# Loading q of the last three batches as zero-padded token rows and transposing it by DMA from SBUF

## The chip, the cores and the metric

The kernel runs on one core of one Trainium2 chip. The metric is the device time of one execution in microseconds (us). Times are medians of several runs; the profile is of one further execution, taken by the hardware profiler.

## What is computed

Eight batches of eight heads, 576 tokens, head size 64: attention in which a token sees itself and the 63 tokens before it. The result, 4608 tokens by 512 columns, goes through two matrix products with a function between them.

```python
scores = scale * np.matmul(q, k.transpose(0, 1, 3, 2))
mask = (rel >= 0) & (rel < window)          # window = 64
attn = softmax of np.where(mask, scores, -1e9)
x = np.matmul(attn, v)                      # rearranged to (4608, 512)
h = x @ w_in                                # 512 -> 2048
g = h - np.tanh(h)
out = g @ w_out                             # 2048 -> 512
```

## The kernel before

**Tiling.** A pair g is two heads of one batch (g = 4b + pair, pairs 0 to 31). A batch is cut into nine windows of 64 tokens; a window of queries meets 128 keys. The dense part works on nine chunks of 512 tokens. A batch has 576 tokens, so chunk c needs parts of batches c-1 and c. All of PSUM is one tile of eight banks: 0 to 2 hold the dense products, 3 the transposes, 4 the scores, 5 to 7 the products with v (for batch 0, banks 0, 1 and 7 serve otherwise too).

**The order is written out.** `PLAN` is a list of some 1300 words; each calls one function of the table `STEPS`, and what it issues goes into the queue of its engine in that order. An engine takes its instructions strictly in the order of the list, and waits at the first whose data or buffer isn't ready. Words that matter here (the last letter of some is the engine: v VectorE, a ScalarE, p GpSimd):

- `H.c.m` four products of 512 columns into one bank (L487), `A.c.m` tanh (L495, ScalarE), `G.c.m` the subtraction (L501, VectorE), which frees the bank. In chunk 0 `H.0.m` uses bank m mod 3, in chunk 1 (m+1) mod 3, later m mod 2.
- `W.c.s.p` four products with w_out (L526); 128 tokens s take four of them. `O.c.s` copies the result out of PSUM (L88 or L90) and stores it by a DMA from the SP queue (L542). The last 128 tokens are done in two halves of the columns (L519, L537).
- `Rp.g.n.4` three score products of 128 columns for three windows into bank 4 (L300), `Rx.g.n.4` exp of them (L305, ScalarE), `M.g` masking (L393, VectorE), `PP.g` the products with v for two pairs (L418), `DR` and `DN` their normalization (L426, L435, L438).
- Batches 0 to 2 bring k to the layout that `Rp` needs by PE: a load, a cast (`ck`), six transposes (`Fp`, L261), a copy out of PSUM (`Fc`). For q the same: `cq`, `Ep.g.3`, and two copies `Ea`, `Eb` (64 partitions each, L88 or L90), since q lies in a buffer padded with zeros so that one product serves both heads. Transposes and their copies share bank 3.
- Batches 3 to 7 load k as token rows, `lr.b.i.h` (L176): block i of 128 tokens (the fifth has 64), four heads h; `tk.b.i` (L181) then transposes the block by DMA from SBUF, issued by SP.
- q of batches 3 to 7 is loaded by one DMA per batch, `LQ.b` (L114). Batches 3, 4 and 5 go through PE (`cq`, `Ep`, `Ea`, `Eb`). Batches 6 and 7 go, per pair, through `cz.g` (two copies on GpSimd into a zeroed tile, L128), `bo.g` (a DMA to a DRAM buffer, L133) and `td.g` (a DMA transpose from DRAM, L138).
- `LV.b.i` loads v (L160), `Z.b` copies it across partitions (L166, L167). `Y.b` transposes the attention's result into the dense part's input by two DMAs (L472); for batches 0 to 2 PE does it (`Xp`, `Xc`).
- `wi` and `wo` load the weights (L189, L197); `U` is a product on zeros, `N` puts the mask into bank 6 (L245).

**Queues.** GpSimd issues all loads with a cast; SP issues the outputs, the DMA transposes and the bounce. The transposed q has two buffers (pairs g mod 2).

Of the kernel before, what the change touches and what calls it, by code (L numbers as in the profile page):

```python
# [15 lines left out]
def kernel(  # L16
# [69 lines left out]
    def move(eng, o, i):  # L86
        if eng is nc.scalar:
            nc.scalar.activation(o, i, ACT.Copy)  # L88
# [35 lines left out]
    def cast_q(g):  # L124

        i = stage.pop((g, "q")).rearrange("p h (e d) -> p h e d", d=D)
        for h in range(2):
            nc.gpsimd.tensor_copy(qz[g % 2][:, h, :, 64 * h:64 * h + 64], i[:, h])  # L128

    def bounce(g):  # L130

        t = dram.tile([2, S, 128], BF16, tag="q", name="qd")
        nc.sync.dma_start(out=t.rearrange("h (p e) c -> p h (e c)", e=E),  # L133
                          in_=qz[g % 2].rearrange("p h e c -> p h (e c)"))
        rows[g, "qd"] = t

    def tr_dma(g):
        nc.sync.dma_start(out=qT[g % NR].rearrange("c h s -> c (h s)"),  # L138
                          in_=rows.pop((g, "qd")).rearrange("h s c -> (h s) c"), transpose=True)
# [414 lines left out]
    def subtract(c, m, s=None):  # L554
# [18 lines left out]
        P=pv, D=norm, PP=pv_pairs, DR=recip_pairs, DN=norm_pairs, Xp=x_tr, Xc=x_put, Y=x_dma,  # L573
        H=first_layer, A=tanh, G=subtract, W=yp_mm, O=y_out)

    def play(script):
# [16 lines left out]
        H.0.6 Rp.4.1.4 G.0.4 A.0.6 Fc.6.3.a G.0.6 wo.2 wo.3 H.0.8 cq.6.v lq.9.p H.0.7 lk.9.p cq.7.v H.0.9 A.0.8  # L593
        G.0.8 A.0.7 lv.1.3.0 G.0.7 Ep.7.3 A.0.9 G.0.9 H.0.11 Eb.7.3.a Rx.4.1.4 A.0.11 za.1.0.v lv.1.2.0 Ea.7.3.v
        lv.1.2.1 H.0.10 H.0.12 lv.1.3.1 Rp.7.2.4 G.0.11 lr.3.3.0 A.0.10 lk.10.p G.0.10 Ep.6.3 A.0.12 Eb.6.3.a
        lq.11.p Ea.6.3.a G.0.12 H.0.14 A.0.14 H.0.13 LV.2.1 Rx.7.2.4 M.4 H.0.15 lk.11.p Rp.6.0.4 M.5 Rx.6.0.4
        PP.4 G.0.14 A.0.15 lq.10.p zb.1.3.p cq.8.v LQ.3 DR.4 G.0.15 Rp.7.0.4 LV.2.0 Rx.7.0.4 W.0.0.0 Rp.6.2.4
        A.0.13 DN.4.0 W.0.0.1 ck.8.v Ep.8.3 Rx.6.2.4 Rp.6.1.4 Rx.6.1.4 LV.2.3 Ea.8.3.v Eb.8.3.v G.0.13 W.0.1.0
        M.6 W.0.0.2 Rp.7.1.4 W.0.1.1 DN.4.1 Fp.8.3 W.0.1.2 W.0.0.3 LV.2.2 Rx.7.1.4 lr.3.3.1 cq.9.v Fc.8.3.a
        Rp.8.2.4 Rx.8.2.4 O.0.0.v Ep.9.3 Ea.9.3.a Eb.9.3.a W.0.1.3 W.0.2.0 O.0.1.a ck.9.v Fp.9.3 M.7 Rp.8.0.4  # L600
        W.0.2.1 Rx.8.0.4 W.0.3.0 DN.4.2 lr.3.2.1 Fc.9.3.a zb.1.2.v Xp.1.0.0.3 za.1.2.v lr.3.4.1 Xc.1.0.0.3.a
        Rp.9.2.4 za.1.3.v ck.10.v PP.6 lr.3.1.0 DR.6 Xp.1.0.1.3 DN.6.1 lr.3.4.0 tk.3.3 LV.2.4 DN.6.2 lr.3.1.1
# [103 lines left out]
```

## Time and profile before

| | us |
|---|---|
| median of 3 runs (315.44 to 316.02) | 315.92 |
| profiled execution, its own time | 314.95 |
| span of its trace | 313.3 |
| PE busy | 302.4 (97%) |
| VectorE busy | 187.8 (60%) |
| ScalarE busy | 171.2 (55%) |
| GpSimd busy | 108.6 (35%) |
| granted TensorE clock | 0.998 |

Busy times are unions of an engine's instructions within the span; the time outside the span (some 1.7 us) belongs to the start and the end of the execution. Matmuls are pipelined: four products of 512 columns are shown as 1.03 us when they stand alone, but follow each other every 0.86 us.

### The profile page before, as it was taken

To read this page: it belongs to the slowest core of one execution; us is meant where nothing else is said; L and a number is where in the kernel's file an instruction comes from. 1 tells how busy PE (TensorE), PEld (TensorE's weight loads), DVE (VectorE), ACT (ScalarE), POOL (GpSimd) and SP (SyncE) were. 2 spreads that over 40 slices of the span, in tenths; PEclk is the share of its full clock that TensorE was granted. 3 is DMA by queue.
4 is the path that set the end of the run, shared out by engine and by line. 5 is a ranking of instruction groups with operands and counts; after the bars stand their busy time and mean duration, and the time that the engine had idled before them with its cause. 6 is when DMAs were issued, how large, how long until landed. Compare 5 with 4: busy or idle time off the path is not lost.

```text
span 313.3 us, 6081 instructions
## 1 busy us (share of the span) xinstructions
PE 302.4 (97%) x2385; PEld 165.0 (53%) x2413; DVE 187.8 (60%) x327; ACT 171.2 (55%) x320; POOL 108.6 (35%) x160
## 2 busy tenths in 40 slices
PE   6988999999999999999999999999999999999995
PEld 2564565656655555555555455555554444444444
DVE  3685988699758785667556555873774534343300
ACT  3576875489866767657454536445333533433311
POOL 8990666686739442293441640000000000000000
PEclk9999999999999999999999999999999999999999
DMA  9999999999999999997999999481005110010111
GB/s 158 149 181 203 170 208 137 192 138 141 142 116 151 143 156 159 127 132 170 175 183 165 181 193 175 113 180 36 35 36 116 59 37 33 33 37 33 67 69 67
DMA packets 113133, 39.11 MB, mean 125 GB/s; under 512 B 96336, under 2 KB 107600, under 8 KB 113104
## 3 DMA queue, kind: packets, MB, share of 16 engines
q0 software_dynamic: 72064, 18.06, 67.1%
q1 hardware_dynamic: 41040, 20.65, 30.5%
q8 instruction: 19, 0.31, 0.4%
q14 instruction: 10, 0.08, 0.1%
HBM read 36.70 MB, written 11.80 MB: 155 GB/s over the span
## 4 chain that ended last, share of the span: by engine, by line
PE 87%; DMA 5%; POOL 5%; issue 1%; ACT 0%; POOLq 0%; ACTq 0%
PE ps L487 39%; PE ps L526 37%; PE ps L300 4%; PE ps L418 3%; DMA xT<-xs 3%; DMA wi<-in_moe_w_in_dram 3%; PE ps L261 2%; POOL kall L108 1%; POOL vw L160 1%; POOL qall L108 1%; PE ps L519 1%; PE ps L453 1%; POOL vw L147 0%; POOL seen L241 0%; ACT ysb L88 0%
## 5 line engine op out<-in xcount | busy, mean ns | idle before, releaser
L501 DVE TENSOR_TENSOR gT<-ps,th 128x512 bf16<-128x512 f32 x144 | 97.3, 687 | 81.9 <-ACT th L495 81.2
L487 PE MATMUL ps<-xT,wi 128*128 128x512 bf16 x576 | 141.7, 379 | 1.1 <-DMA wi<-in_moe_w_in_dram 0.7
L526 PE MATMUL ps<-w_out_sb,gT 128*128 128x512 bf16 x532 | 131.8, 379 | 1.4
L495 ACT ACTIVATE th<-ps 128x512 f32<-128x512 f32 x144 | 84.6, 597 | 77.8 <-PE ps L487 75.6
L487 PEld LDWEIGHTS <-wi 128*128 128x128 bf16 x576 | 62.0, 113 | 50.4 <-DMA wi<-in_moe_w_in_dram 0.9
L526 PEld LDWEIGHTS <-gT 128*128 128x128 bf16 x560 | 53.0, 98 | 56.9
L305 ACT ACTIVATE pt<-ps 128x384 bf16<-128x384 f32 (+2 forms) x92 | 45.8, 504 | 20.3 <-PE ps L300 19.0
L176 POOL DMA_DIRECT2D kall<-in_k_dram x50 | 37.2, 758 | 28.2 <-DMA kw<-kall 19.9
L160 POOL DMA_DIRECT2D vw<-in_v_dram x35 | 31.1, 894 | 10.8 <-PE ps L418 8.6
L88 ACT ACTIVATE ysb<-ps 128x512 f32<-128x512 f32 (+1 forms) x23 | 13.3, 579 | 28.4 <-PE ps L526 25.9
L393 DVE TENSOR_TENSOR pt<-pt,ps 128x1152 bf16<-128x1152 bf16 x28 | 20.6, 745 | 2.7 <-ACT pt L305 2.7
L300 PEld LDWEIGHTS <-kw 128*128 128x128 bf16 x180 | 14.4, 98 | 11.7 <-issue 0.3
L88 ACT ACTIVATE qt<-ps 64x576 bf16<-64x576 bf16 x30 | 19.3, 642 | 1.3 <-PE ps L300 0.3
L300 PE MATMUL ps<-qt,kw 128*128 128x128 bf16 x180 | 19.0, 219 | 0.0
L128 POOL COPY qz<-qall 96x384 bf16<-96x384 bf16 x16 | 7.6, 528 | 24.9 <-DMA qd<-qz 11.6
L438 DVE TENSOR_TENSOR xs<-ps,rcp 128x384 bf16<-128x384 f32 x28 | 14.9, 548 | 0.1
L225 PE MATMUL ps<-warm 128*128 128x512 bf16 x26 | 9.3, 496 | 2.2 <-DVE warm L206 2.1
L90 DVE COPY ysb<-ps 128x512 f32<-128x512 f32 x14 | 9.6, 685 | 3.1 <-PE ps L526 3.1
L418 PEld LDWEIGHTS <-pt 128*64 128x64 bf16 x504 | 9.2, 112 | 3.0 <-issue 1.3
L418 PE MATMUL ps<-vw,pt 128*64 128x65 bf16 x504 | 10.7, 197 | 0.0
L261 PE MATMUL ps<-ident,qb 96*128 96x96 bf16 x132 | 9.3, 206 | 1.0 <-DVE qb L90 1.0
L261 PEld LDWEIGHTS <-qb 96*128 96x128 bf16 x132 | 7.5, 97 | 4.5 <-DVE qb L90 1.9
(69 smaller groups left out, 165.4 us busy)
## 6 DMA issues: line engine op xcount, KB each, us to landing
out_dram<-ysb SPq DMA_DIRECT2D x35, 256.0 KB, 2.2
vw<-in_v_dram POOLq DMA_DIRECT2D x28, 128.0 KB, 5.3
qall<-in_q_dram POOLq DMA_DIRECT2D x5, 576.0 KB, 8.7
kall<-in_k_dram POOLq DMA_DIRECT2D x40, 64.0 KB, 4.8
qd<-qz SPq DMA_DIRECT2D x8, 288.0 KB, 3.3
w_out_sb<-in_moe_w_out_dram POOLq DMA_DIRECT2D x4, 512.0 KB, 8.4
kall<-in_k_dram POOLq DMA_DIRECT2D x11, 144.0 KB, 4.7
qall<-in_q_dram POOLq DMA_DIRECT2D x11, 144.0 KB, 4.6
```

The costliest lines, as they stand in the source:

```text
L88: nc.scalar.activation(o, i, ACT.Copy)
L160: nc.gpsimd.dma_start(out=w[:, 2 * i + 1, :, 0:D] if i < NF else w[64:128, 2 * i, :, 0:D], in_=v[b, :, 128 * i:128 * i + n].rearrange("h p ...
L176: nc.gpsimd.dma_start(out=token_rows(b)[0:c, i, :, h, :], in_=k[b, NP * h:NP * h + NP, 128 * i:128 * i + c].rearrange("r p d -> p r d"))
L261: nc.tensor.transpose(tp[:, e, :], src[:, e, :], ident[:P, :P])
L300: nc.tensor.matmul(sp[:, i], kt[:, 64 * j:64 * j + 128], qT[g % NR][:, :, 64 * j:64 * j + 64], start=first, stop=first or i == n - 1)
L305: nc.scalar.activation(PT[g % NPT][:, js[0]:js[0] + len(js), :].rearrange("p i (h t) -> p i h t", h=2), sp, ACT.Exp, scale=scale)
L393: nc.vector.tensor_tensor(p, p, mask.unsqueeze(1).to_broadcast([128, 2 * NJ, 64]), ALU.mult)
L418: nc.tensor.matmul(ps[r, bank, 65 * i:65 * i + 65], PT[(g + r2) % NPT][:, j, r], vw[b % 2][:, j, p0 + r2 + NP * h, :], start=True, stop=True)
L487: nc.tensor.matmul(hp, w_in_tile(ki, m), chunk_tile(c)[:, n.start // 64:n.stop // 64, ki % 2, 64 * (ki // 2):64 * (ki // 2) + 64], start=( ...
L495: nc.scalar.activation(th[:, n], hp, ACT.Tanh)
L501: nc.vector.tensor_tensor(gT[c][:, m, columns(s)], hp, th, ALU.subtract)
L526: nc.tensor.matmul(yp, gT[c][:, m, s * 128:(s + 1) * 128], w_out_sb[:, m, :], start=n == 1 and i == 0, stop=n == 4 and i == 3)
```

## The change

1. q of batches 5, 6 and 7 takes one path. `Lq.b.half.i` (30 DMAs by GpSimd) loads a block of 128 tokens, four heads, into every second half of zeroed rows; `tq.b.two.i` (30 DMA transposes by SP) turns a block of two pairs into the padded layout. `LQ.5` to `LQ.7`, `cq`, `Ep`, `Ea`, `Eb` of pairs 20 to 23, and `cz`, `bo`, `td` of pairs 24 to 31 go, with the DRAM buffer.
2. The transposed q has four buffers, one for each pair of a batch, in one tile; the rows of q have one buffer. Two more memsets (`mq.2`, `mq.3`).
3. The zeroing `z` is in five words, one for each block of rows: 128x1024 bf16 each in place of two of 96x1536.
4. P.2 writes banks 0 and 1; its normalization is in three instructions (`DS.2`, `DH.2.0`, `DH.2.1`) in place of two.
5. The last 128 tokens are cut into 128 and 384 columns, the 384 last, in place of two halves of 256.
6. The list is as it was up to `D.2`, and in a new order from there. One of the nine `U` words is dropped, and the engine of some copies and casts is another.

```diff
-    qT = [const.tile([128, 2, S], BF16, name=f"qt{i}") for i in range(NR)]
+    q_two = const.tile([128, NP, 2, S], BF16, name="qt0")
+    qT = [q_two[:, i] for i in range(NP)]
+    q_rows = const.tile([128, NF + 1, NP, 2, 128], BF16, name="qr0")
-    qz = [const.tile([P, 2, E, 128], BF16, name=f"qz{i}") for i in range(2)]
...
+    def load_q_rows(b, half, i):
+        c = min(128, S - 128 * i)
+        nc.gpsimd.dma_start(out=q_rows[0:c, i, :, half, 64 * half:64 * half + 64],
+                            in_=q[b, NP * half:NP * half + NP, 128 * i:128 * i + c].rearrange("r p d -> p r d"))
+    def tr_q(b, two, i):
+        c = min(128, S - 128 * i)
+        nc.sync.dma_start(out=q_two[:, 2 * two:2 * two + 2, :, 128 * i:128 * i + c].rearrange("p r h c -> p (r h) c"),
+                          in_=q_rows[0:c, i, 2 * two:2 * two + 2].rearrange("p r h d -> p (r h d)"), transpose=True)
...
     def more_zeros(i):
-        nc.vector.memset(qz[i], 0.0)
+        nc.vector.memset(q_rows[:, i], 0.0)
...
     def pv_banks(g):
-        return ps[:, 4:8:3, :] if g < NP and g % 2 and not BY_HEAD else ps[:, 5:7, :]
+        return ps[:, 0:2, :] if g == 2 else ps[:, 5:7, :]
...
+    def norm_sums(g):
+        ov = pv_banks(g)[:, :, 0:5 * (D + 1)].rearrange("p n (i c) -> p n i c", c=D + 1)
+        last[g] = sm_pool.tile([128, 2, 5, 1], F32, tag="rc", name="rc")
+        nc.vector.reciprocal(last[g], ov[:, :, :, D:D + 1])
+    def norm_half(g, n):
+        b, pr = divmod(g, NP)
+        k = 5 - n
+        ov = pv_banks(g)[:, n, 0:k * (D + 1)].rearrange("p (i c) -> p i c", c=D + 1)
+        nc.vector.tensor_tensor(xs[b % 2][:, 5 * n:5 * n + k, pr, :], ov[:, :, 0:D],
+                                last[g][:, n, 0:k].to_broadcast([128, k, D]), ALU.mult)
...
+    def last_columns(half):
+        n = 3 * d_model // 4
+        return slice(0, n) if half else slice(n, d_model)
```

The stretches of the list that the prediction speaks of, before and after. First, where the dense part begins:

```diff
-        Rx.5.0.4 lv.1.0.1 lv.1.0.0 Xp.0.0.0.3 Rp.5.1.4 D.2 Xc.0.0.0.3.a U.1.2 Xp.0.1.0.3 Xp.0.1.1.2 Rx.5.1.4
-        Xc.0.1.1.2.v U.1 mq.0 Rp.5.2.4 Xc.0.1.0.3.a H.0.1 A.0.1 H.0.0 ck.7.v Rx.5.2.4 G.0.1 H.0.2 wo.0 za.1.1.p
-        lq.8.p A.0.0 G.0.0 A.0.2 Ep.4.3 H.0.4 Eb.4.3.a wo.1 Ea.4.3.a A.0.4 ck.6.v G.0.2 H.0.3 Fp.7.3 Rp.4.2.4
-        lk.8.p H.0.5 A.0.3 N Fc.7.3.v zb.1.0.p Rx.4.2.4 G.0.3 Fp.6.3 A.0.5 zb.1.1.p Rp.4.0.4 Rx.4.0.4 G.0.5
+        Rx.5.0.4 lv.1.0.1 lv.1.0.0 Xp.0.0.0.3 Rp.5.1.4 DS.2 DH.2.0 DH.2.1 Xc.0.0.0.3.a U.1.2 Xp.0.1.0.3
+        Xp.0.1.1.2 Rx.5.1.4 Xc.0.1.1.2.v U.1 mq.0 lq.8.p N mq.3 Rp.5.2.4 mq.2 Xc.0.1.0.3.a lk.8.p Ep.4.3 ck.7.v
+        Rx.5.2.4 Ea.4.3.a ck.6.v H.0.1 A.0.1 Eb.4.3.a H.0.0 A.0.0 G.0.0 H.0.2 z.4 A.0.2 Rp.4.2.4 z.2 Rx.4.2.4
+        Rp.4.0.4 G.0.1 za.1.1.p Rx.4.0.4 wo.1 H.0.3 Fp.7.3 H.0.4 wo.0 G.0.2 cq.7.v A.0.3 Rp.4.1.4 wo.2 Rx.4.1.4
+        Fc.7.3.v Fp.6.3 A.0.4 H.0.5 G.0.3 A.0.5 lq.9.p G.0.4 H.0.6 zb.1.1.p Fc.6.3.v G.0.5 H.0.7 Ep.7.3 A.0.6
+        G.0.6 A.0.7 Ea.7.3.a wo.3 Eb.7.3.a H.0.8 lv.1.3.0 A.0.8 H.0.9 zb.1.0.p A.0.9 lk.9.p cq.6.v Rp.7.2.4
+        lv.1.3.1 G.0.7 G.0.8 Ep.6.3 G.0.9 H.0.10 Ea.6.3.a Rx.7.2.4 lv.1.2.0 M.5 A.0.10 G.0.10 cq.8.a Eb.6.3.v
+        lv.1.2.1 H.0.11 H.0.12 A.0.11 G.0.11 H.0.13 Ep.8.3 lk.11.p A.0.12 Eb.8.3.a LV.2.1 Rp.6.0.4 za.1.0.v
+        G.0.12 M.4 H.0.14 H.0.15 A.0.14 G.0.14 PP.4 Rx.6.0.4 ck.8.a W.0.0.0 Ea.8.3.v Rp.7.0.4 W.0.0.1 DR.4
```

Second, the first transposes of batches 5 and 6 (only the words of the SP and GpSimd queues and a few of PE are kept):

```
SP:     O.2.0 tq.5.0.1 tq.5.0.4 tk.5.1 tq.5.0.3 tk.5.4 tq.5.0.0 tk.5.0 tq.5.0.2 tk.6.2 tq.5.1.4 O.2.1 tq.5.1.3
        tq.5.1.1 tq.5.1.2 tq.5.1.0 Y.4 O.2.2 tq.6.0.1 tk.6.4 O.2.3 tq.6.0.2 tq.6.1.2 tk.6.1 O.3.0 tq.6.0.3
        tk.6.0 tq.6.1.0 tq.6.0.0 tq.6.1.3 O.3.1 tq.6.1.1 tq.6.1.4 tq.6.0.4 tk.6.3 Y.5 O.3.2
GpSimd: lr.7.1.1 LV.5.2 LV.5.4 lr.6.0.0 lr.6.0.1 Lq.6.0.0 LV.5.0 LV.5.3 Lq.6.0.1 Lq.6.0.2 LV.6.3 lr.6.1.0
        lr.6.4.1 Lq.6.1.1 Lq.6.1.2 lr.7.4.0 lr.6.3.1 lr.6.1.1 Lq.6.1.3 Lq.6.0.3
```

Third, the end:

```diff
-        W.8.0.2 G.8.15 W.8.1.2 W.8.0.3 W.8.1.3 O.8.0.a W.8.2.0 W.8.2.1 W.8.2.2 W.8.2.3 W.8.3.2 O.8.1.a W.8.3.3
-        O.8.2.a W.8.3.0 W.8.3.1 O.9.0.a O.8.3.a"""
+        G.8.15 W.8.0.0 W.8.0.1 W.8.0.2 W.8.0.3 W.8.1.1 W.8.1.2 O.8.0.a W.8.1.3 O.8.1.a W.8.2.0 W.8.2.1 W.8.2.2
+        W.8.2.3 O.8.2.v W.8.3.0 W.8.3.1 W.8.3.2 O.8.3.a W.8.3.3 O.9.0.a"""
```

More of the change, by code (lines that the diff above doesn't have):

```diff
@@ L109, in load, with load_q @@
         stage[g, n] = t
-    def load_all(b, n):
-        t = rows_all[n][b % 2][0:P]
-        nc.gpsimd.dma_start(out=t, in_=(q if n == "q" else k)[b].rearrange("h (p e) d -> p h (e d)", e=E))
+    def load_q(b):
+        t = rows_all["q"][b % 2][0:P]
+        nc.gpsimd.dma_start(out=t, in_=q[b].rearrange("h (p e) d -> p h (e d)", e=E))
         for pr in range(NP):
-            stage[b * NP + pr, n] = t[:, pr::NP]
+            stage[b * NP + pr, "q"] = t[:, pr::NP]
     def cast(g, n, eng=nc.gpsimd):
@@ L122, in cast @@
         rows[g, n] = t
[L124 to L139, printed above, removed]
+    def load_q_rows(b, half, i):
[6 more added lines that the diff above has]
+                          in_=q_rows[0:c, i, 2 * two:2 * two + 2].rearrange("p r h d -> p (r h d)"), transpose=True)
     def load_v_tail(b, eng=nc.gpsimd):
@@ L271, in put @@
             r = slice(64 * h, 64 * h + 64)
-            move(eng, qT[g % NR].rearrange("c h (p e) -> c h p e", e=E)[r, h], t[r])
+            move(eng, qT[g % NP].rearrange("c h (p e) -> c h p e", e=E)[r, h], t[r])
     def group(g, grp, bank):
@@ L299, in scores @@
         for i, j in enumerate(js):
-            nc.tensor.matmul(sp[:, i], kt[:, 64 * j:64 * j + 128], qT[g % NR][:, :, 64 * j:64 * j + 64],
+            nc.tensor.matmul(sp[:, i], kt[:, 64 * j:64 * j + 128], qT[g % NP][:, :, 64 * j:64 * j + 64],
                              start=first, stop=first or i == n - 1)
@@ L447, in norm @@
         nc.vector.tensor_tensor(xo[:, :, :, pr, :], ov[:, :, :, 0:D], rc.to_broadcast([128, 2, 5, D]), ALU.mult)
+    last = {}
+    def norm_sums(g):
[8 more added lines that the diff above has]
+                                last[g][:, n, 0:k].to_broadcast([128, k, D]), ALU.mult)
     def x_tr(b, half, part, bank):
@@ L514, in yp_mm @@
             half = part // 2
-            d = slice(half * (d_model // 2), (half + 1) * (d_model // 2))
+            d = last_columns(half)
             n = turn(c, s, half)
@@ L532, in y_out @@
             c, s = NC - 1, 3
-            d = slice(half * (d_model // 2), (half + 1) * (d_model // 2))
+            d = last_columns(half)
             ysb = sm_pool.tile([128, d_model], F32, tag="ysb", name="ysb")
@@ L558 @@
         i=make_ident, u=make_warm, mv=pads_v, mt=pads_k, mq=pads_q, mk=pads_kw, U=warm_up, h=make_hide, n=make_mask, N=put_mask,
-        z=lambda: [more_zeros(i) for i in range(2)],
+        z=more_zeros,
         lk=lambda g, e: load(g, "k", e), lq=lambda g, e: load(g, "q", e),
-        LK=lambda b: load_all(b, "k"), LQ=lambda b: load_all(b, "q"),
+        LQ=load_q, Lq=load_q_rows,
         lt=load_v_tail, lv=load_v, LV=load_rows,
@@ L593 @@
[L593 to L602, printed above, removed]
@@ new lines @@
+        Xc.1.0.0.3.a za.1.2.v W.0.2.2 PP.6 Xp.1.0.1.3 DR.6 DN.6.0 lr.3.3.0 lr.3.2.1 DN.6.2 ck.10.v ck.11.a
+        Rx.9.2.4 Xc.1.0.1.3.a W.0.3.0 W.0.3.1 lr.3.4.0 Xp.1.1.0.3 Xc.1.1.0.3.a z.1 W.0.2.3 cq.10.a DN.6.1
+        Xp.1.1.1.3 Rp.8.0.4 W.0.3.2 Rx.8.0.4 Rp.9.1.4 Xc.1.1.1.3.v Rx.9.1.4 tk.3.2 Ep.10.3 LV.2.4 H.1.0 A.1.0
+        Ea.10.3.v O.0.2.v G.1.0 W.0.3.3 Eb.10.3.a lr.3.1.0 H.1.1 Fp.10.3 Rp.8.1.4 cq.11.a lr.3.1.1 A.1.1 O.0.3.v
+        Rx.8.1.4 Fc.10.3.a Z.2 H.1.2 H.1.3 A.1.2 A.1.3 G.1.1 G.1.2 lr.3.0.1 Fp.11.3 Rp.9.0.4 H.1.4 G.1.3
@@ new lines @@
+        Rx.9.0.4 M.8 A.1.4 M.9 Fc.11.3.a lr.3.0.0 Rp.10.2.4 Rx.10.2.4 tk.3.3 tk.3.1 G.1.4 z.3 lr.3.4.1 H.1.5
+        H.1.6 Rp.10.0.4 Ep.11.3 A.1.5 lr.5.2.1 LV.3.2 A.1.6 Eb.11.3.a G.1.5 H.1.7 Ea.11.3.a H.1.8 cq.14.v G.1.6
+        Rx.10.0.4 A.1.7 LV.3.4 LV.3.1 lr.4.3.0 cq.13.v Rp.10.1.4 PP.8 A.1.8 G.1.7 cq.12.a Rx.10.1.4 LQ.4 H.1.9
+        Ep.12.3 Rp.11.1.4 A.1.9 LV.3.0 lr.4.3.1 G.1.8 DR.8 Rx.11.1.4 Ea.12.3.a DN.8.2 LV.3.3 H.1.10 G.1.9
+        Eb.12.3.a tk.3.4 H.1.11 DN.8.0 A.1.10 lr.4.0.1 Rp.11.0.4 H.1.12 A.1.11 Ep.13.3 lr.4.2.0 cq.15.v
@@ new lines @@
+        Rx.17.2.4 Rp.16.2.4 Ea.19.3.a O.1.3.a M.17 Z.4 Rx.16.2.4 H.2.14 lr.5.0.0 A.2.13 lr.5.1.1 Rp.16.1.4
+        W.2.0.0 lr.7.2.1 A.2.14 Rx.16.1.4 G.2.13 W.2.0.1 Eb.19.3.v G.2.14 tk.5.3 Rp.18.1.4 H.2.15 A.2.15
+        Lq.5.1.4 W.2.0.2 G.2.15 lr.6.2.0 Rx.18.1.4 H.3.0 H.3.1 lr.5.0.1 A.3.0 Rp.18.0.4 G.3.0 W.2.0.3 H.3.2
+        A.3.1 Rx.18.0.4 Rp.19.1.4 M.16 Lq.5.0.3 G.3.1 O.2.0.a lr.5.4.1 H.3.3 A.3.2 PP.16 lr.6.4.0 Rx.19.1.4
+        Rp.18.2.4 Lq.5.0.0 A.3.3 tq.5.0.1 G.3.2 DR.16 H.3.4 G.3.3 A.3.4 W.2.1.0 Lq.5.1.2 Rx.18.2.4 M.18 tq.5.0.4
@@ new lines @@
+        tq.6.0.4 DR.22 A.4.11 DN.22.2 DN.22.0 Lq.7.1.1 G.4.10 H.4.12 G.4.11 W.3.2.3 DN.22.1 Rp.25.0.3 tk.6.3
+        H.4.13 Rx.25.0.3 A.4.13 A.4.12 Y.5 O.3.2.v Lq.7.1.4 LV.6.1 W.3.3.0 Rp.24.1.3 Lq.7.0.3 Lq.7.0.1 G.4.12
+        W.3.3.1 W.3.3.2 Rx.25.1.4 Rp.24.0.4 G.4.13 Rx.24.0.4 H.4.15 H.4.14 A.4.15 A.4.14 Rp.26.2.4 W.3.3.3
+        LV.6.0 G.4.15 Rx.24.1.3 lr.7.0.1 Rx.26.2.4 H.5.1 G.4.14 O.3.3.a Rp.25.2.3 LV.7.0 Rx.25.2.3 lr.7.1.0
+        Rp.24.2.4 Lq.7.1.3 Rx.24.2.4 W.4.0.0 M.24 H.5.0 A.5.0 W.4.0.1 W.4.0.2 LV.6.2 Lq.7.0.4 G.5.0 W.4.0.3
@@ new lines @@
+        G.5.8 M.27 tk.7.4 H.5.10 LV.7.3 tq.7.0.4 PP.26 tq.7.0.2 G.5.11 A.5.10 G.5.10 O.4.2.a tq.7.1.3 H.5.13
+        A.5.13 DR.26 DN.26.1 H.5.12 W.4.3.0 W.4.3.1 DN.26.2 W.4.3.2 DN.26.0 LV.7.2 A.5.12 LV.7.1 G.5.12 LV.7.4
+        Y.6 H.5.14 W.4.3.3 G.5.13 Rp.29.2.3 O.4.3.a H.5.15 Z.7 Rp.29.1.4 A.5.14 Rx.29.1.4 G.5.14 W.5.0.0
+        Rx.29.2.3 W.5.0.1 tq.7.1.1 Rp.29.0.3 A.5.15 H.6.0 G.5.15 H.6.1 Rx.29.0.3 A.6.0 Rp.28.0.4 A.6.1 W.5.0.2
+        Rp.28.1.3 G.6.0 G.6.1 H.6.2 Rx.28.0.4 H.6.3 M.29 Rx.28.1.3 Rp.28.2.4 tq.7.1.0 A.6.2 W.5.0.3 G.6.2
```

132 lines of the change are left out of this document (57 added, 75 removed).

## The prediction, on record before the result

> **What bounds the kernel.** I read the page first: busy times, slices, the chain that ended last.
>
> ```profile
> PE 302.4 (97%) x2385; PEld 165.0 (53%) x2413; DVE 187.8 (60%) x327; ACT 171.2 (55%) x320; POOL 108.6 (35%) x160
> ...
> PE   6988999999999999999999999999999999999995
> ...
> ACT  3576875489866767657454536445333533433311
> ...
> PEclk9999999999999999999999999999999999999999
> ...
> PE 87%; DMA 5%; POOL 5%; issue 1%; ACT 0%; POOLq 0%; ACTq 0%
> ```
>
> PE is busy in every slice after the third, at full clock, and holds 87% of the chain. A busy matmul can hide waits, so I also added up PE's work along the list: four 512-column products 0.865 us (rows of L487 and L526 that follow each other), three score products 0.17, a pair of pairs in L418 0.90, six transposes 0.26. From 26.0 us, when the dense part begins, this gives 309.7 for the last matmul; the trace has 309.8. So PE has under 1 us of waits after 26 us: anything that adds a wait there is paid in full. The timeline shows where it begins and its largest later wait:
>
> ```profile
> 26.00 2.78 PE L487 MATMUL ps<-xT,wi 128*128 128x512 bf16 x12 [0.72 <-DMA wi<-in_moe_w_in_dram]
> 27.09 0.60 ACT L495 ACTIVATE th<-ps 128x512 f32<-128x512 f32 x1 [1.83 <-PE ps L487]
> ...
> 29.44 1.30 ACT L88 ACTIVATE qt<-ps 64x576 bf16<-64x576 bf16 x2
> ```
>
> ```profile
> 110.80 0.42 PE L261 MATMUL ps<-ident,qb 96*128 96x96 bf16 x6
> ...
> 118.13 1.92 PE L487 MATMUL ps<-xT,wi 128*128 128x512 bf16 x8 [0.27 <-DMA xT<-xs]
> ```
>
> The first line is the wait for w_in; the last is H.3 waiting for Y.3, whose DMA was issued at 109.42 and landed 8.7 us later.
>
> **The change, part by part.**
>
> *PE work.* Four Ep words go: six transposes begin at 110.80 and the next product at 111.06, so 4 x 0.26 = 1.04. One U of 512 columns goes: 0.22. Ep.4 (0.26) and N (0.13, 32.17 to 32.30) move ahead of H.0.1, into the wait that ends at 26.00. Sum: -1.65 us. The casts, copies and bounces that go were beside PE's work, and cost nothing.
>
> *Y.3.* DN.14, which it needs, comes 1.3 us earlier in PE's positions, and H.3 0.6 earlier; GpSimd stands still before it (lr.7.2.1 waits for tk.5.2), so fewer loads are in flight. The wait of 0.27 and the restart of a drained pipe (four products 1.03 instead of 0.86) go: -0.44.
>
> *The first chunk, 26 to 45 us.* New waits. H.0.1, H.0.0, H.0.2 end at 28.59, Rp.4.2 at 28.76. The next word on PE, Rp.4.0, writes the same bank 4 with nothing between (before, three words lay between). It waits for Rx.4.2 on ScalarE, which stands behind A.0.1, Eb.4, A.0.0 and A.0.2: 27.09 + 0.60 + 0.65 + 0.60 + 0.60 + 0.49 = 30.03. Wait: 1.3. Then Rp, H.0.3, Fp.7, H.0.4, Rp take PE to 32.4, and Fp.6 needs bank 3 from Fc.7 on VectorE, whose queue from A.0.0's end (28.95) holds G.0.0 0.69, two of the new memsets, G.0.1 and G.0.2 0.66 each, cq.7 0.38 and Fc.7 0.76. A memset of 128x1024 bf16 isn't in the trace; 128x1152 took 0.538 and 128x256 0.165, so 0.48. Sum: 33.1, wait 0.7. From Ea.7 (36.7) on ScalarE has no pause, since cq.8 (0.83 there, 0.40 on VectorE) has come to it; H.0.13, H.0.15 and PP.4 wait for subtractions behind it, together 0.9. In all 2.9, against 0.4 now (PP.4 due at 42.1 by the sum, begun at 42.50): **+2.5**. Bounds: the first wait alone less the 0.4, +0.9; all of them and those of W.0, +3.2.
>
> *55 to 87 us.* By the rows' durations the list gives ScalarE 29.9 us of work for PE's 30 between positions 55 and 85 (27.3 before), VectorE 28.7 (28.3), as ck.8, ck.11, cq.11 and cq.12 moved to ScalarE and two memsets came. Today's waits there are 0.35. +0.5, bounds 0 and +1.5.
>
> *The loads and transposes.* No Lq or tq is in the trace; the nearest rows are k's.
>
> ```profile
> kall<-in_k_dram POOLq DMA_DIRECT2D x40, 64.0 KB, 4.8
> ...
> kw<-kall SPq DMA_TRANSPOSE x25, 4.2
> ```
>
> ```profile
> qall<-in_q_dram POOLq DMA_DIRECT2D x5, 576.0 KB, 8.7
> ```
>
> Lq: same size and runs as lr, 0.76 of GpSimd and 4.8 to land (2.5 to 9.7 seen); tq: same shape as tk, one every 1.31 on SP (94.80, 96.11, 97.48) and 4.2 to land (2.4 to 8.1). GpSimd gains 30 x 0.76 and loses 3 x 0.80 + 16 x 0.53, +12 us; it is 35% busy. In-order waiting is what matters. Rp.20.2 (position 133.3) needs tk.5.4: O.2.0 goes out at about 122, tk.5.4 is the fifth transpose behind it, issued at 127, landed 131. Y.4 stands behind 14 transposes: 122 + 18.3 + 0.4 = 141, landed 3.4 later (Y.4's latency now) 144.4; H.4 is due at 144.9. Lq.6.0.0 overwrites rows that tq.5.1.0 reads, so GpSimd stops until that lands, about 143.5; behind it LV.5.0, LV.5.3 (needed at 153). Lq.6.1.1 is the ninth load, issued at 150, landed 154.5; SP stands at tq.6.0.1 until then, and the outputs behind it have three buffers, enough. From there 14 transposes and three outputs bring Y.5 to 174, landed 177.5; H.5.1 is due at 177, tk.6.3 lands at 176 for Rp.26.2 due at 175.9. All due times move on by the early waits, as O.2.0 does. Covers of 0.5 to 1 us: +0.4, bounds 0 and +4.5. If this cover fails, PE waits, since H and Rp stand in PE's order. In GpSimd's later stops (Lq.7 behind tq.6) LV.6.2 lands near 187 for Z.6 at 190.
>
> Against LQ's replacement speaks a rule of the Trainium skill, page DMA: Bandwidth & Descriptors, section Rules for kernel authors: coalesce many small transfers into a large one, since those under 64 KB are mostly overhead. The rows differ: behind others, LQ.3 landed 4.5 us after its predecessor, four lr within 1.0 (65.79 to 66.75), so ten small ones take no longer than one large. By the page's fixed cost of about 2 us, ten in a row would take an estimated 20 us, and the sum would be that of the late-loads rival below.
>
> *q's buffers.* Four instead of two only relax; the padding's memsets are priced above, mq.2 and mq.3 fall into VectorE's pause before 27. P.2 in other banks is before 26 us, hidden by w_in's landing.
>
> *The end.* 16 products of 128 and 16 of 384 columns take as long as 32 of 256 (0.056 + 0.163 against 2 x 0.109). The last copy grows from 256 to 384 columns: 0.38 to 0.49 (the row of 128x384). Its store, 192 KB, lies between 1.7 (128 KB) and 2.0 (256 KB): 1.85. +0.26; bounds 0.1 and 0.4.
>
> Sum: -1.65 - 0.44 + 2.5 + 0.5 + 0.4 + 0.26 = +1.57. The profiled execution took 314.95 (span 313.3 and 1.65 around it), so 316.5; the median of the runs is 0.97 above it: **317.5**.
>
> **The rivals.**
>
> *Only the bank-4 wait is real (faster).* One mechanism: a follower on ScalarE costs less than its row, since two tanh in a row took 1.06 and not 1.20. With 0.07 saved per follower the queues behind Fc.7 and Ea.7 keep up, the 0.7 and 0.9 vanish, and so does the +0.5 later. -1.65 - 0.44 + (1.3 - 0.4) + 0.26 = -0.93: **315.0**. It decides at early waits of under about 1.8 us. For it: before is just as full (ScalarE 17.8 of 19 us between 26 and 45) and lost 0.4. Against: the first two waits are chains of single instructions, not a matter of fill.
>
> *The loads come late.* Lq.6.1.1 takes 9.1 us as lr did at 98.91, not 4.5. tq.6.0.1, and all SP issues up to Y.5, come 4.6 later, and H.5 waits 4: **321.5**. Against: GpSimd has stood idle just before, so few loads are in flight.
>
> *Nothing shows.* The gains meet half of the waits: 316.
>
> *It doesn't do what it says:* if waits went by whole tiles, Rp.22.1 would wait for tq.6.0.1, 14 us. Banks of the one PSUM tile are used side by side now, so I leave it out.
>
> **How the numbers follow.** The forecast's kind (slower by 0.7 to 3) 0.49, late loads 0.13, nothing shows 0.14, faster 0.24. A measurement of this kernel tells about 0.2%, 0.6 us, from no change. So faster 0.24, same 0.14, slower 0.62. The range leaves out the lowest tenth, where the early waits are absent (313.7 at the bound), and the worst of late loads: 314.6 to 320.6. The likeliest case alone has 316.6 to 319.
>
> **What would show it.** Right: in the timeline after, a PE wait of about 1.3 at 28.8 us ended by ScalarE's exp; PP.4 near 45; no wait at Y.3; 26 us for H.0.1 as now; the last matmul near 311. Wrong: PP.4 before 43.5 (then the early term), idle GpSimd under 10 us near 133 to 143 (then the load chain), or a new PE wait on DMA xT or qt above 1 us.

## The result and the profile after

The changed kernel takes **319.17 us** in the median of six runs (318.58 to 320.30); the kernel before, run beside it, takes 315.65 (314.98 to 316.02). The ratio is 1.0122, interval 1.0094 to 1.0150: **slower by 3.5 us**, where 1.6 were forecast. The profiled execution took 320.16 us, with a span of 318.4 and a granted clock of 0.995; that of before took 314.95 with 313.3, so these two are 5.2 us apart: the profiled execution of before was faster than all six of its runs, that of after 1 us slower than the median of its own.

From the page after, the lines that answer to those of before:

```profile
PE 303.1 (95%) x2360; PEld 163.7 (51%) x2388; DVE 189.1 (59%) x327; ACT 169.1 (53%) x314; POOL 120.4 (38%) x171
...
PE   5998999999999999989999899999999999999995
...
PEclk9799999999999999999999999999999999999999
...
PE 75%; DVE 6%; DMA 6%; ACT 4%; POOL 3%; issue 2%; SPq 2%; POOLq 0%; DVEq 0%; ACTq 0%
```

PE's row now has an 8 in two late slices, 135 to 143 us and 175 to 183 us, and PE holds 75% of the chain, not 87%: the end is now set through other queues too. One slice of the clock shows a 7; that is another matter (last section). The timeline names the places. The columns are start, length, engine, line, operation; in brackets how long PE stood still before, and what ended it:

```profile
26.53 2.76 PE L496 MATMUL ps<-xT,wi 128*128 128x512 bf16 x12
...
30.51 0.33 PE L295 MATMUL ps<-qt,kt 128*128 128x128 bf16 x3 [1.05 <-ACT pt L300]
...
33.51 0.42 PE L256 MATMUL ps<-ident,kb 96*128 96x96 bf16 x6 [0.33 <-DVE kt L90]
...
45.13 0.76 PE L413 MATMUL ps<-vw,pt 128*64 128x65 bf16 x36
...
139.68 0.34 PE L295 MATMUL ps<-qt,kw 128*128 128x128 bf16 x3 [1.42 <-DMA kw<-kall]
...
183.66 0.84 PE L496 MATMUL ps<-xT,wi 128*128 128x512 bf16 x3 [1.52 <-DMA xT<-xs]
```

These are H.0.1, Rp.4.0, Fp.6, PP.4, Rp.20.0 (which waits for tk.5.0) and H.5.1 (which waits for Y.5). The first waits were forecast; the last two are the surprise. Put into the terms of the forecast, in us:

| | forecast | measured | how |
|---|---|---|---|
| start of the dense part | 0 | +0.53 | H.0.1 at 26.00, now 26.53 |
| PE work | -1.65 | -1.65 | 32 fewer PE instructions after H.0.1: 5 words of six transposes, N, one U |
| Y.3 | -0.44 | -0.43 | no wait between 98 and 139 |
| first chunk | +2.5 | +2.2 | H.0.1 to PP.4: 16.50, now 18.60, with 0.13 less work between |
| 46 to 100 us | +0.5 | +0.9 | waits above 0.06: 0.4, now 1.3 |
| loads and transposes | +0.4 | **+3.2** | 1.5 near 140 and 1.7 near 184, each with the restart of the pipe |
| end | +0.26 | +0.36 | last product's start to the span's end: 3.77, now 4.13 |
| small gaps, not placed | | +0.1 | |
| sum | +1.57 | +5.2 | |

A wait is counted from start to start of two products, beyond their usual spacing; gaps of 0.22 us at which the trace lacks a product are left out. The terms add up to the 5.2 us of these two executions, not to the 3.5 of the medians.

One term is wrong by far, and it is so in the second profile of the changed kernel as well (2.7, experiment 1). The next lines are of the GpSimd queue and the SP queue there:

```profile
130.63 0.76 POOL L171 DMA_DIRECT2D kall<-in_k_dram  x1 [10.67 <-DMA kw<-kall]
131.37 1.59 POOL L155 DMA_DIRECT2D vw<-in_v_dram  x2
132.92 1.53 POOL L171 DMA_DIRECT2D kall<-in_k_dram  x2
146.20 0.74 POOL L127 DMA_DIRECT2D qr<-in_q_dram  x1 [11.74 <-DMA qt<-qr]
```

```profile
131.54 1.23 SPq L133 DMA_TRANSPOSE qt<-qr  x1
132.87 1.23 SPq L176 DMA_TRANSPOSE kw<-kall  x1
...
147.79 0.37 SPq L555 DMA_DIRECT2D out_dram<-ysb  x1
158.18 1.20 SPq L133 DMA_TRANSPOSE qt<-qr  x1
```

GpSimd stands at lr.7.1.1 until tk.5.1 lands (130.08), and then issues five loads in 4 us. In the middle of them SP issues tq.5.0.0 and tk.5.0 (131.54, 132.87). These land at 138.34 and 139.63, 6.8 us after their issue; tq.5.0.1 and tk.5.1, issued from 125 on with no load beside them, took 2.4. Then GpSimd stands 11.74 us at Lq.6.0.0, whose rows tq.5.1.0 still reads, and SP issues nothing for 10.0 us (148.16 to 158.18) before tq.6.0.1, whose rows come with Lq.6.1.1 (issued 152.37, landed 158.04). Y.5 is seventeen issues later: 179.68, landed 183.61.

### The profile page after: what moved, and what is told of

Its sections match the earlier page's. It is cut to its first block, busy times and chain, and to the rows that moved or that the text cites. A ratio compares the mean times of both kernels' runs of the same rounds, so it can differ in the third digit from the quotient of the medians.

```text
span 318.4 us, 6058 instructions
## 1 busy us (share of the span) xinstructions
PE 303.1 (95%) x2360; PEld 163.7 (51%) x2388; DVE 189.1 (59%) x327; ACT 169.1 (53%) x314; POOL 120.4 (38%) x171
## 4 chain that ended last, share of the span: by engine, by line
PE 75%; DVE 6%; DMA 6%; ACT 4%; POOL 3%; issue 2%; SPq 2%; POOLq 0%; DVEq 0%; ACTq 0%
PE ps L539 34%; PE ps L496 31%; PE ps L295 3%; DMA kw<-kall 3%; DVE gT L510 3%; PE ps L413 2%; DMA kall<-in_k_dram 2%; ACT th L504 2%; ACT qt L88 2%; SPq L133 1%; POOL vw L155 1%; DMA xT<-xs 1%; PE ps L256 1%; PE ps L532 1%; PE ps L462 1%
## 5 line engine op out<-in xcount | busy, mean ns | idle before, releaser
L171 POOL DMA_DIRECT2D kall<-in_k_dram x50 | 37.7, 767 | 32.6 <-DMA kw<-kall 20.3
L127 POOL DMA_DIRECT2D qr<-in_q_dram x30 | 22.4, 755 | 27.6 <-DMA qt<-qr 26.2
L88 ACT ACTIVATE ysb<-ps 128x512 f32<-128x512 f32 (+2 forms) x22 | 12.7, 579 | 26.3 <-PE ps L539 20.1
L90 DVE COPY ysb<-ps 128x512 f32<-128x512 f32 x15 | 10.3, 687 | 14.6 <-PE ps L539 14.5
L88 ACT ACTIVATE qt<-ps 64x576 bf16<-64x576 bf16 x23 | 14.7, 641 | 1.1 <-PE ps L256 0.4
L108 POOL DMA_DIRECT2D kall<-in_k_dram x11 | 7.7, 703 | 5.6 <-DMA qall<-in_q_dram 2.3
L256 PE MATMUL ps<-ident,qb 96*128 96x96 bf16 x108 | 7.6, 206 | 1.9 <-DVE qb L90 1.9
```

The source lines that it names most:

```text
L127: nc.gpsimd.dma_start(out=q_rows[0:c, i, :, half, 64 * half:64 * half + 64], in_=q[b, NP * half:NP * half + NP, 128 * i:128 * i + c].rearr ...
L171: nc.gpsimd.dma_start(out=token_rows(b)[0:c, i, :, h, :], in_=k[b, NP * h:NP * h + NP, 128 * i:128 * i + c].rearrange("r p d -> p r d"))
```

## The experiments

Each kernel is the changed one with the edit shown, unless another is named; its label stands in brackets. Ratios are to the kernel before, run beside it, with their 95% intervals; the changed kernel had 1.0122 (1.0094 to 1.0150).

**1. The changed kernel again (a_again).** No edit.

> The changed kernel once more, unchanged, beside the others on one chip. Theory: the two late waits of PE belong to the order of the queues and not to one execution, so the second profile shows them again: about 1.4 us near 140 us, ended by kw (tk.5.0), and about 1.5 near 184, ended by xT (Y.5); the dense part's start at 26.5 instead of 26.0 and the eighth of the granted clock missing in the second slice are one execution's, and vary. Time 318.6 to 320.3. Rival: the late waits are one execution's luck with its DMAs; then one of them is under 0.5 here, and the time at full clock is under 318.

Ratio 1.0116 (1.0083 to 1.0148). H.0.1 at 26.24, the waits 0.95 at 30.1, 0.33 at 33.1, 1.16 at 138.9 and 1.22 at 182.6; the clock was 1.0 throughout. The late waits belong to the order, and make 2.7 us with restarts here.

**2. The burst alone (x_burst).**

```diff
-  lr.7.1.1 LV.5.2 LV.5.4 lr.6.0.0 lr.6.0.1
+  LV.5.2 LV.5.4 lr.6.0.0 lr.6.0.1 lr.7.1.1
```

> One GpSimd word moved: lr.7.1.1, which waits for tk.5.1, goes behind LV.5.2, LV.5.4, lr.6.0.0 and lr.6.0.1, so that these four are issued at 120 to 123.5 us and not in a burst at 131 to 134. Theory: the burst, let go when tk.5.1 lands, shares the DMA engines with tq.5.0.0, tk.5.0 and tq.5.0.2 and makes them land 6 to 7 us after their issue instead of 2.5; without it tk.5.0 lands by 136.5, the PE wait of 1.4 (1.6 with the restart) near 140 goes, and the time falls by 1.6, to about 317.6. Rival: tk.5.0 is late since it stands seventh in the SP queue, 1.31 us apart; then the wait stays above 1 us and the time within 0.4 of the changed kernel's.

Ratio 1.0168 (1.0128 to 1.0207): not faster. The mechanism came out as expected: tk.5.0, issued at 132.97, landed at 136.90, and no PE wait stands near 140. But PE then arrives earlier at what comes next:

```profile
180.45 0.34 PE L295 MATMUL ps<-qt,kw 128*128 128x128 bf16 x3 [0.62 <-DMA kw<-kall]
...
183.04 1.05 PE L496 MATMUL ps<-xT,wi 128*128 128x512 bf16 x4 [1.39 <-DMA xT<-xs]
```

Y.5 landed at 183.00, as late as ever, and what was saved at 140 was lost at 180. My expectation counted the two waits as separate costs. They are one: SP's chain runs from O.2.0 to Y.5 in its own time, and PE can't pass its end.

**3. A second buffer for the rows of q (x_rows2).** Batch 6 gets rows of its own, in the room of the staged q.

```diff
-    out=q_rows[0:c, i, :, half, ...]
+    out=q_block(b, i)[0:c, :, half, ...]   # batch 6: rows_all["q"]
+  z.5 z.6 z.7 z.8 z.9
```

> Batch 6 gets rows of its own for q, in the room of the staged q of batches 3 and 4, zeroed by five more memsets; nothing else moves. Lq.6 no longer waits for tq.5. Theory: GpSimd goes on at about 135 us instead of standing until 146, tq.6.0.1 is issued behind O.2.2 near 148 instead of 158, Y.5 long before 177, and the PE wait of 1.5 (1.7 with the restart) near 184 goes: 1.6 less, about 317.6, if the earlier loads don't lengthen the wait near 140. They may: nine loads more while tk.5.0 is under way add up to 1 us there, then 318.6. Rival: SP's one transpose every 1.31 us is what makes Y.5 late, not the rows; then the wait near 184 stays above 1 us.

Ratio 1.0247 (1.0201 to 1.0292): slower still, though GpSimd went on at 133.5, Y.5 was issued at 176.5 and the wait near 184 went. The wait for tk.5.0 stayed (1.00 at 138.8). The loads now ran beside tq.5 and Y.4, and PE waited for these. tq.5.1.0 took 7.1 us to land, Y.4's first half too:

```profile
149.23 0.27 PE L301 MATMUL ps<-qt,kw 128*128 128x128 bf16 x2 [1.20 <-DMA qt<-qr]
...
152.51 1.05 PE L502 MATMUL ps<-xT,wi 128*128 128x512 bf16 x4 [1.11 <-DMA xT<-xs]
```

**4. No loads Lq for batches 6 and 7 (x_nolq).**

```diff
-  Lq.6.* Lq.7.*     # all 20 words that begin so
```

> Leaves out the 20 loads Lq of batches 6 and 7, so that their attention is computed with the q of batch 5; the transposes tq stay, all 30. Theory: GpSimd no longer stands at Lq.6.0.0, SP no longer at tq.6.0.1: tq.6.0.1 behind O.2.2 at 148, Y.5 issued near 170, the wait near 184 gone, the wait near 140 (the burst of k and v loads) left: 1.5 less than the changed kernel. Rival: the transposes alone, 15 of tq and 5 of tk beside Y, fill the SP queue, and Y.5 is late without any Lq: then the wait near 184 stays above 1 us.

Ratio 1.0252 (1.0203 to 1.0301). The wait near 140 stayed and the one near 184 went, as the theory had it, but the time went the other way, which neither theory nor rival has. With nothing to stop it at Lq.6.0.0, GpSimd issued 14 loads of k and v from 139 to 150 us, beside tq.5 and Y.4:

```profile
149.83 0.27 PE L295 MATMUL ps<-qt,kw 128*128 128x128 bf16 x2 [0.81 <-DMA qt<-qr]
...
153.78 1.06 PE L496 MATMUL ps<-xT,wi 128*128 128x512 bf16 x4 [1.78 <-DMA xT<-xs]
```

Y.4's first half, issued at 145.79, landed at 153.73. So what makes a transpose late is not the loads of q as such but any loads in flight beside it, and GpSimd's long stop, which I had read as harm alone, also keeps the way free.

**5. The first chunk in the order of before (x_hyb).**

```diff
-  H.0.1 A.0.1 Eb.4.3.a H.0.0 A.0.0 G.0.0 H.0.2 z.4 A.0.2 Rp.4.2.4 z.2 Rx.4.2.4 Rp.4.0.4 ...
+  H.0.1 A.0.1 H.0.0 ck.7.v Rx.5.2.4 G.0.1 H.0.2 ... A.0.0 G.0.0 A.0.2 Ep.4.3 H.0.4 Eb.4.3.a ...
```

> The words from D.2 to W.0.0.0 in the order and on the engines of the kernel before, the rest as in the changed one; two memsets of q's rows go behind DR.4. Theory: the early waits (2.5 us near 30.5, 33.5, 43 to 44) go, those of before (0.2) come, Ep.4 and N return behind the first dense products (0.39): 1.9 less, about 317.3; PP.4 begins at 42.5 to 43 and no PE wait above 0.3 lies between 27 and 43. Rival: the waits move behind W.0.0.0, since ScalarE and VectorE have the same work to do by 60 us in either order: within 0.7 of the changed kernel, 318.5 or more.

Ratio 1.0211 (1.0187 to 1.0236), of no use as a time: where I joined the two orders I put Eb.8 on ScalarE ahead of Rx.7.0, and PE stood 2.52 us at 48.6 for it. The stretch before the join says what was asked: H.0.1 to PP.4 took 16.8 us (18.6 in the changed kernel, 16.5 before), and no PE wait above 0.2 lies in it. The early waits are a matter of the order of that stretch and of the engines of its copies, which both went back here; experiment 6 changes the order alone.

**6. The first chunk repaired (x_early).**

```diff
-  H.0.1 A.0.1 Eb.4.3.a H.0.0 A.0.0 G.0.0 H.0.2 z.4 A.0.2 Rp.4.2.4 z.2 Rx.4.2.4 Rp.4.0.4 G.0.1 za.1.1.p Rx.4.0.4 wo.1 H.0.3 Fp.7.3 H.0.4 ...
+  H.0.1 A.0.1 Eb.4.3.a H.0.0 G.0.1 A.0.0 H.0.2 Rp.4.2.4 Rx.4.2.4 G.0.0 A.0.2 za.1.1.p wo.1 H.0.4 Fp.7.3 Fc.7.3.v Rp.4.0.4 A.0.4 Rx.4.0.4 H.0.3 ...
```

> Only the first chunk is reordered: G.0.1 before G.0.0, H.0.4, Fp.7 and their copies between Rp.4.2 and Rp.4.0, Rx.4.2 ahead of A.0.2, mq.0 a little earlier, z.2 and z.4 behind DR.4. Theory: the waits at 30.1 (0.95) and 33.1 (0.33) with their restarts go, 1.6 in all, and the stores up to O.2.0 go out 1.4 to 1.6 earlier. SP's row of transposes starts behind O.2.0, so what comes after moves with it, and most of it reaches the end: 1.2 to 1.6 less than the changed kernel, about 317.5 beside 318.9. Rival: the loads for batches 5 and 6 come when they come; then PE only waits longer near 140 and 184 (1.5 more together), and the time stays within 0.4 of the changed kernel.

Ratio 1.0083 (1.0050 to 1.0115). H.0.1 to PP.4 took 17.0 us: 1.6 saved there.

```profile
29.22 0.33 PE L295 MATMUL ps<-qt,kt 128*128 128x128 bf16 x3
29.39 1.03 PE L496 MATMUL ps<-xT,wi 128*128 128x512 bf16 x4
30.25 0.42 PE L256 MATMUL ps<-ident,kb 96*128 96x96 bf16 x6
30.51 0.33 PE L295 MATMUL ps<-qt,kt 128*128 128x128 bf16 x3
```

Rp.4.2 (29.22) and Rp.4.0 (30.51) now have H.0.4 and Fp.7 between them, and no wait. Of the 1.6 us 0.9 were left at O.2.0 (a wait of 0.49 for VectorE stood at 94), and 0.5 over the whole way from H.0.1 to the last product (286.47, against 286.96 in experiment 1): the waits near 139 and 182 stayed at 1.35 and 1.20. By the ratios it is about 1 us under the changed kernel, but the two intervals overlap. Theory and rival both hold in part.

**7. GpSimd's order (x_pool).** LV.5 and lr.6 at 117 to 124 us, Lq.6 from block 1 on.

```diff
-  lr.7.1.1 LV.5.2 LV.5.4 lr.6.0.0 lr.6.0.1 Lq.6.0.0 LV.5.0 LV.5.3 Lq.6.0.1 Lq.6.0.2 ... lr.6.1.0 lr.6.4.1 Lq.6.1.1 ...
+  LV.5.2 LV.5.4 lr.6.0.0 lr.6.0.1 LV.5.0 LV.5.3 lr.6.1.0 lr.6.4.1 lr.7.1.1 ... Lq.6.0.1 Lq.6.1.1 Lq.6.0.2 ... Lq.6.0.0 Lq.6.1.0
```

> Only GpSimd's order of 27 loads is changed: LV.5 and four of lr.6, which wait for nothing, fill its idle time from 119 us, lr.7.1.1 comes behind them, and Lq.6 begins with block 1 of both halves, which tq.6.0.1 needs, and ends with block 0, which tq.5.1.0 holds longest. Theory: tq.6.0.1 is issued near 150 instead of 158, Y.5 near 172 and not 179, the wait near 184 goes (1.4 to 1.7); the wait near 140 goes or falls below 0.5, since no burst follows tk.5.1; 2 to 3 less than the changed kernel, about 316.5. Rival: any load beside the transposes makes these late, wherever it stands; then waits of 1 us or more appear between 125 and 155, and the time falls by under 1.

Ratio 1.0092 (1.0056 to 1.0127), an interval that overlaps with the changed kernel's. tq.6.0.1 went out at 149.85, Y.5 at 174.72, and the wait near 184 went. But Lq.6, issued from 143.80 on, was now in flight beside Y.4 (issued 144.78, landed 150.29), as the rival had it: a wait of 1.78 us stood at 150.3.

**8. Both (x_both).**

> x_early and x_pool together. Theory: the two terms add up, 1.5 and 2.5: 4 less than the changed kernel, about 315, which is the time of the kernel before within 0.5. Rival: what one saves the other loses, 317 or more.

Ratio 1.0037 (1.0020 to 1.0055): 2.7 us under the changed kernel. One late wait was left, for Y.4, issued at 142.38 and landed at 147.38 with Lq.6 beside it from 141.41 on:

```profile
147.42 1.05 PE L496 MATMUL ps<-xT,wi 128*128 128x512 bf16 x4 [1.30 <-DMA xT<-xs]
```

**9. What the dropped PE work was worth at its place (x_work).**

```diff
+  Rp.19.0.4 U.3.3 ... W.2.2.0 U.2.3
```

> The changed kernel with five products of 512 columns on zeros added on PE, two behind W.2.2.0 and three behind Rp.19.0, at 135 to 138 us: 1.08 us, as much as the four words Ep of pairs 20 to 23 were (1.04), and in their place. Nothing waits for them but PE. Theory: PE stands still for tk.5.0 near 140 anyway, so the wait of 1.2 to 1.4 there falls to 0.1 to 0.4 and the time stays within 0.4 of the changed kernel: what the dropped words saved there brought nothing. Rival: each us of PE's work counts, as the prediction had it: 1.1 more.

Ratio 1.0139 (1.0112 to 1.0166). The interval holds both no change and 1 us more, so the time doesn't decide. The trace, of the fastest of its four executions, shows where the added work went:

```profile
136.34 0.59 PE L220 MATMUL ps<-warm 128*128 128x512 bf16 x2
...
137.95 0.34 PE L295 MATMUL ps<-qt,kw 128*128 128x128 bf16 x3
```

Rp.20.0 (137.95) now waits 0.15 us instead of 1.16 to 1.42, and from H.0.1 to the last product PE took 286.57 us, against 286.96 without the added 1.08. The work saved there had been swallowed by the wait for tk.5.0.

**10. GpSimd held back for Y.4 (x_gate).** x_both with one word moved.

```diff
-  Lq.6.0.1 Lq.6.1.1 Lq.6.0.2 ... Lq.6.0.0 Lq.6.1.0
+  Lq.6.0.0 Lq.6.0.1 Lq.6.1.1 Lq.6.0.2 ... Lq.6.1.0
```

> The reordered kernel of x_both with Lq.6.0.0 first among the Lq.6, so that GpSimd stands until tq.5.1.0 lands (144.3) and Y.4, issued at 142.4, has fewer loads beside it. Theory: Y.4's first half lands by 145.5 instead of 147.4, the wait of 1.3 (1.46 with the restart) near 147 goes; tq.6.0.1 goes out near 150 instead of 147, Y.5 near 174, still in time: 1.2 to 1.4 less than x_both, about 314.7, and 0.2% under the kernel before. Rival: Y.5 then comes late again, and a wait of 1 us or more stands near 180: as x_both.

Ratio 0.9993 (0.9970 to 1.0016). Lq.6.0.0 is released only when tq.5.1.0 lands (144.62), so Y.4 has no Lq beside it until 145.18: issued at 143.53, landed at 146.79. Y.5 was issued at 174.02, in time. PE's waits from 100 us on, first of the changed kernel, then of this one (engine, line, what was waited for; us in total, times, longest):

```profile
PE ps L496 <- DMA xT<-xs: 1.5, 1, 1.5
PE ps L295 <- DMA kw<-kall: 1.4, 1, 1.4
```

```profile
core 0 of [0], span 313.4 us
engine line waited for: us in total, times, longest us
```

The second answer is empty: the whole loss of the late stretch is gone, by order alone.

**11 and 12. What is left (x_best, x_top).** The last 128 tokens in halves again and cq.15 behind G.1.10; then cq.16 behind G.2.3 and Eb.12 behind A.1.10 as well.

```diff
-        n = 3 * d_model // 4
+        n = d_model // 2
-  cq.15.v ... G.1.10
+  G.1.10 cq.15.v
```

```diff
-  cq.16.v ... G.2.3     Eb.12.3.a ... A.1.10
+  G.2.3 cq.16.v         A.1.10 Eb.12.3.a
```

> x_gate with the last 128 tokens in two halves of 256 columns again, and cq.15 behind G.1.10 on VectorE. Theory: the end is 0.25 shorter (the last copy 0.38 instead of 0.49, the last store 128 KB instead of 192), and the wait of 0.3 near 77 goes: 0.5 less than x_gate, about 314.2. Rival: neither can be told in the time; within 0.2 of x_gate.

> x_best with two words moved: cq.16 behind G.2.3 on VectorE and Eb.12 behind A.1.10 on ScalarE, against the two largest waits left on PE (0.34 of standing still at 94.3, 0.16 with the restart at 78.1). Theory: both go, 0.5 to 0.8 less than x_best from the first dense product on, about 314.7 in the median, 0.2% under the kernel before: what is left of the dropped PE work. Rival: the queues of ScalarE and VectorE are full between 70 and 100 us, and the waits only move; then as x_best, no difference from before that can be told.

Ratios 0.9990 (0.9972 to 1.0008) and 0.9986 (0.9956 to 1.0016): neither can be told from the kernel before, nor from x_gate. From H.0.1 to the last product the three took 283.48, 283.36 and 283.46 us, before 283.49. From the last product on, x_best took 3.82 us and x_gate 4.12, so the piece of 384 columns costs 0.3. In x_top the wait that stood at 94.3 in x_best (0.34) only moved, to 95.8 (0.56), as its rival said. No version beats the kernel before by more than the measurement can tell.

## Why the prediction was wrong, step by step

**PE work, -1.65.** Right by count, wrong as a term of the sum: four Ep words lay between O.2.0 and tk.5.0's landing, where PE waited anyway (experiment 9). The prediction's opening, "anything that adds a wait there is paid in full", fits the trace of before. It doesn't follow that each us of work taken out is gained: in the changed kernel some of it stood beside a wait.

**Y.3, -0.44.** Right.

**The first chunk, +2.5.** Right in size (+2.2) and in place. The bank-4 wait was 1.05 and 1.2 with the restart (1.3 forecast), the one for Fc.7 0.33 and 0.5 with it (0.7), those before PP.4 0.4 (0.9); PP.4 began at 45.1 (near 45), half a microsecond of it from the later start of H.0.1. ScalarE's row shows the cause as it was worked out: A.0.0 and A.0.2 stand ahead of Rx.4.2.

```profile
28.99 1.09 ACT L504 ACTIVATE th<-ps 128x512 f32<-128x512 f32 x2
29.96 0.50 ACT L300 ACTIVATE pt<-ps 128x384 bf16<-128x384 f32 x1
```

**55 to 87 us, +0.5; the end, +0.26.** 0.9 (taken from 46 to 100 us) and 0.3 to 0.36, both inside their bounds.

**The loads and transposes, +0.4: this step failed.** It measured +3.2, inside its bounds of 0 and +4.5. It had three faults.

The first: the cover was checked for the wrong transpose. The text has Rp.20.2 safe behind tk.5.4 (it was: 133.22), and never asks for Rp.20.0, which needs tk.5.0, two places later in the SP queue. By the forecast's own times tk.5.0 would have landed half a microsecond before Rp.20.0 was due.

The second, and the cause of the wait near 140: each transpose was given one landing time, 4.2 us for tk and 3.4 for Y, as if it were a property of the transpose. In these traces it depends on what is in flight beside it: tk.5.0 took 6.8 us beside the burst and 3.9 without it (experiment 2). For each DMA transpose from SBUF (tk, tq and Y) issued after 60 us I counted the GpSimd loads in flight 1 us after its issue, and took the mean time to land (in brackets how many):

| loads in flight | before | after |
|---|---|---|
| none | 3.3 us (12) | 2.7 us (25) |
| 1 or 2 | 4.4 (8) | 3.7 (11) |
| 3 to 5 | 5.9 (12) | 5.7 (22) |
| 6 or more | 8.5 (3) | 5.9 (7) |

The left column could be read before the result. With it tk.5.0, sent out among five loads, would have been given 5.9 us, 1.7 more than 4.2; and the list shows the burst, since lr.7.1.1 waits for tk.5.1. The Trainium skill states in DMA: Bandwidth & Descriptors, section Issuing engines are not separate DMA queues, that DMAs from different engines run on the same 16 DMA engines and interleave. This trace agrees in that transposes beside loads land later (5.7 to 5.9 us against 2.7).

The third, and the cause of the wait near 184: the end of a long chain was given next to no cover. From O.2.0 on, the forecast's chain went tq.5.1.0 landed +21.5, Lq.6.1.1 landed +32.5, Y.5 issued +52, landed +55.5 us. Measured, it was +21.1, +33.5, +55.2 and +59.1. Lq.6.1.1 took 5.7 us among its neighbours instead of 4.5. Then 17 issues took 21.5 us instead of 19.5: the three outputs took 0.6 to 0.7 each instead of 0.4, and two transposes (tk.6.1, tq.6.1.0) held SP for 1.7 and 2.0 instead of 1.3. Their rows had landed before; what held them is not shown. Y.5 took 0.4 longer to land. A cover of half a microsecond at the end of a chain of 55 can't be called a cover. That the chain's timing sets this wait is shown by experiments 7 and 10: with tq.6.0.1 sent out 7 and 4 us earlier behind O.2.0 it went.

**The rivals.** The rival "the loads come late" had the place and the sign, not the cause: Lq.6.1.1 was 1.2 us slower than forecast, not 4.6. That 319.2 us lies inside the range is owed to the room left for this rival, not to a mechanism that was foreseen. "Only the bank-4 wait is real" falls, since the wait for Fc.7 came; and its argument that ScalarE before is just as full (17.8 of 19 us) adds up single rows, whereas its busy time there is 15.8. "Nothing shows" falls by the time. "It doesn't do what it says" was rightly left out: Rp.22.1 ran at 148.1, 10 us before tq.6.0.1 was issued. The rule of the Trainium skill on many small transfers (DMA: Bandwidth & Descriptors, section Rules for kernel authors) isn't what slows this change: the ten Lq.6 of x_gate, in a row, were issued from 145.18 on and had all landed at 155.11. That is 9.9 us, against 8.7 for LQ.6 as one transfer in the trace of before, and not the 20 estimated by that page's fixed cost.

**The signs.** That GpSimd's idle time near 140 would be over 10 us was right (11.7), and it was no proof of the chain; a PE wait on xT above 1 us came, the sign set for wrong. H.0.1 at 26.5 instead of 26.0 is not the change's doing (last section).

**The dropped work.** x_gate has 1.65 us less PE work and no late wait, and yet takes as long as before. Its waits above 0.06 us from 27 us on add up to 2.7, all of them before 103 us and half of them before 46; those of before add up to 1.1, 0.4 of it at Y.3. The difference of 1.6 is the dropped work: what the change saved on PE is lost again in small waits of the first third. Taking the largest of them away only moved them (x_top). What stays open is whether an order without them exists, and what held tk.6.1 and tq.6.1.0.

## What to carry to other kernels

A DMA's time to land is to be read from the rows with as many transfers in flight as it will have, not from the median. Where one in-order queue feeds another (loads, transposes, stores), sum the chain to its end and compare it with the bound engine's sum to the same point: a wait taken away in the middle comes back at the end if the chain ends later. An idle issuing queue can be what keeps the transfers beside it fast, so filling it needs as much care as emptying it.
